# Packed bfloat16 constants in two loads, an earlier query load, more zero products and a later load of the first unit's rows

## The chip, the cores and the metric

The kernel runs on one core of a Trainium2 chip. The metric is the device time of one execution in microseconds (us). The core has the matmul engine (TensorE, PE in the rows; its weight loads are listed as PEld), VectorE (DVE), ScalarE (ACT), GpSimd (POOL) and SyncE (SP), which issues most of the transfers. Each engine works through its own instructions in order and meets the others only through semaphores.

## The reference, cut to what matters

```python
# 1. windowed attention, 2 batches x 8 heads x 768 positions x 64
k_sum = k.reshape(B, H, nb, 32, D).max(axis=3)
v_sum = v.reshape(B, H, nb, 32, D).mean(axis=3)
scores = concat(where(|i - j| < 16, q @ k.T / 8, -1e9), q @ k_sum.T / 8 + log(32))
x = softmax(scores) @ concat(v, v_sum)          # 1536 tokens x 512
# 2. mixture of 8 experts, one expert a token
logits = x @ w_gate;  e = argmax(logits);  gate = softmax(logits)[e]
y = gate * (relu(x_e @ w1[e]) @ w2[e])          # 512 -> 1024 -> 512
# 3. a dense block
h = y @ w_in                                    # 512 -> 2048
out = elu(h) @ w_out                            # 2048 -> 512
```

## The kernel before, in words

The order of all instructions is written out by hand. There are three phases. The first does the attention in 24 steps (12 tiles of 128 positions, two head groups `g` each; the loop over `n`, with `steps[n] = (i, g)`); the second does the experts in units of 384 rows; the third does the dense block in groups of 384 rows.

**A step of attention.** `stage_s` writes the mask into PSUM (a matmul of `ident_b` by the mask, L536), adds the logarithm (L538) and adds 16 score products of the queries `qts[i]` (L543). `stage_x` takes the maximum on DVE (L555 to L562) and the exponentials on ACT (L567). One step later `stage_t` transposes (L584) and two steps later `stage_o` multiplies by the values (L595, then L606 on DVE). After the stages of step `n` come the gate functions of earlier tiles (lists EARLY, MID and LATE), then `late(n)`, which prepares what comes: keys of later tiles, loads, weights.

**The opening.** SP issues the keys of pairs 0 and 1, the constants `cst` (1045 columns of four bytes by 128 rows), the keys of pairs 2 and 3, the queries of tile 0, four parts of the values of batch 0 (`load_vt`, 384 KB each), the queries of tile 1 and the windows of values. Meanwhile PE does WARM products of a zero tile (L752). ACT turns five constants into bfloat16 (`ident_b` L758, three masks L760, `logs` L761), and DVE a sixth (`tri_b`, L813, in `late(0)`). In step 1 and 2 the means of blocks of values are formed: sums on DVE (L911) and POOL (L909), products with `means` (`block_means`, L503), and in between zero products (`keep_clock`, L523); DVE and ACT then copy the means into the value windows (`put_means`, L508 and L509). DVE's `late(1)` converts the capacity (L819) before the first of these copies.

**From attention to the first unit.** Every tile's gate sends its 128 rows into a DRAM buffer `xdisp`, by an indirect store from POOL (`put`, L723; `gate_6` calls it). The first unit is the expert of token 0; `first_unit` is a generator whose pieces (`fill_pe`) are put between instructions of the last steps. It begins with transposes of the rows `XROW0` (L272). `load_rows` (L224) fetches them from `xdisp` in three transfers on SP in `late(X_AT)`; the first of them waits for all puts made so far. A put that comes after it in the program waits for the load, since both touch `xdisp`. In `late(22)`, `load_rows` (if X_AT is 22) stands ahead of the loads of later weights, and behind `gate_6(7)`, which puts tile 7.

**Conversions.** Both weights of the dense block arrive as 64-bit numbers; 32 chunks are turned into float32 on DVE in three instructions each (L406, L409, L400), and after the third the next chunk's load is issued on SP (L381). Chunks 0 to 5 are popped one instruction at a time in `stage_x` and `stage_o` (`fill_in`). What is left, and chunks 6 to 10, stand in the list `conv_tail`. It is popped at numbered places: at place `p` the entry `POINTS[p]` gives ten times the number of pieces of the first unit, plus the number of conversion instructions. Places 0 to 9 lie in steps 22 and 23, 10 to 30 behind the entries of `tail` (place 8 follows `gate_4(9)`, 19 follows `gate_3(10)`, 20 follows `gate_1(11)`), and 31 to 33 in the code that makes the lists of units. What is left of `conv_tail` then is popped in `rest_of_first` (`aside`), one for each piece.

Of the kernel before, what the change touches and what calls it, by code (L numbers as in the profile page):

```python
# [11 lines left out]
BF16 = mybir.dt.bfloat16  # L12
# [11 lines left out]
NB = S // BLK  # L24
# [4 lines left out]
P = 128  # L29
TQ = 64  # L30
WK = TQ + 2 * WIN
NK = WK + NB
# [19 lines left out]
def _consts():  # L52
# [4 lines left out]
    def add(name, a):  # L57
# [3 lines left out]
        cols.append(full)  # L61

    p = np.arange(P)
    add("ident", np.eye(P, dtype=np.float32))
    q = p[:, None] % TQ
    n = np.arange(WK)[None, :]
# [3 lines left out]
    for name, ok in (("mid", band), ("first", first), ("last", last)):  # L70
        m = np.zeros((P, NK), np.float32)
        half = (p[:, None] < TQ) == (name == "first")
        m[:, :WK] = np.where(np.where(half, ok, band), 0.0, NEG)
        add(name, m)

# [5 lines left out]
    for r in (0, D):  # L81
        m[r : r + 3] = np.array(parts, np.float32)[:, None]
    add("logs", m)
    m = np.zeros((P, NK), np.float32)
    m[p[: S // 8], WK + p[: S // 8] // (BLK // 8)] = 1.0 / BLK
    add("means", m)
    add("tri", (p[:, None] < p[None, :]).astype(np.float32))
    add("rev8", np.broadcast_to(E - np.arange(E, dtype=np.float32), (P, E)))
# [23 lines left out]
def moe_chain_kernel(  # L112
# [32 lines left out]
    wg = cp.tile([P, KD, E], F32, name="wg")  # L145
    tri_b = cp.tile([P, P], BF16, name="tri_b")
    ones_b = cp.tile([P, P], BF16, name="ones_b")
# [198 lines left out]
    W_AT = (9, 11, 13, 15, 17, 19, 21, 23)  # L346
    X_AT = 20
    A_AT = (15, 21)
    POINTS = (0, 0, 0, 0, 1, 1, 0, 0, 30, 0, 11, 11, 0, 1, 0, 22, 0, 22, 0, 30, 10, 10, 0, 0, 10, 0, 10, 0, 0, 0, 0, 20, 40, 53)
    WARM = 23  # L350
    PROLOGUE = 2
# [70 lines left out]
    with ExitStack() as att:  # L422
# [87 lines left out]

        masks = fx.tile([P, 3, NK], BF16, name="masks")
        ident_b = fx.tile([P, P], BF16, name="ident_b")
        logs = fx.tile([P, 4, NB], BF16, name="logs")
        OPS = BANK[4].rearrange("p (g u d) -> p g u d", g=2, u=4)
# [17 lines left out]
        def stage_s(i, g):  # L532
            t = i % TPB
            mask = masks[:, 1 if t == 0 else 2 if t == TPB - 1 else 0, :]
            sp = BANK[g][:, 0 : 4 * NK].rearrange("p (u n) -> p u n", u=4)
# [3 lines left out]
                sp[:, :, WK:NK], ones_b[g * D : g * D + 3, :], logs[g * D : g * D + 3], start=False, stop=False  # L539
            )  # L540
            for u in range(4):
                for j in range(2):
                    nc.tensor.matmul(  # L543
                        sp[j * TQ : (j + 1) * TQ, u, :],
                        qts[i][rows, u, j * TQ : (j + 1) * TQ],
                        kws[i][rows, u, j, :],
                        start=False,
                        stop=(u == 3),
                    )
# [190 lines left out]
        load_k(0, 1, 1)  # L740
        nc.sync.dma_start(cst, consts)
        load_k(0, 2, 1)
        load_k(0, 3, 1)
        load_q(0)
        for m in range(4):
            load_vt(0, m)
        load_q(1)
        load_vx(0)
        load_vx(1)

        for _ in range(WARM):
# [5 lines left out]
        block_max(0, 1)  # L757
        nc.scalar.copy(ident_b, ident)  # L758
        for n, name in enumerate(("mid", "first", "last")):
            nc.scalar.copy(masks[:, n, :], C(name))  # L760
        nc.scalar.copy(logs, C("logs").unsqueeze(1).to_broadcast([P, 4, NB]))  # L761
        put_kw(0, nc.scalar.copy, slice(2, 4))
# [40 lines left out]
        def late(n):  # L803
# [6 lines left out]
            if n == 0:  # L810
                nc.sync.dma_start(wg, w_gate.rearrange("p (k e) -> p k e", e=E))
                nc.sync.dma_start(cap_raw, capacity.to_broadcast([P, 1]))
                nc.vector.tensor_copy(tri_b, C("tri"))  # L813
                nc.vector.memset(ones_f, 1.0)
# [629 lines left out]
```

## Time and profile before

| what | us |
|---|---|
| median of 3 runs | 445.79 |
| lowest and highest of these | 445.54 and 449.44 |
| the profiled execution: its own time | 446.14 |
| the profiled execution: span of its trace | 444.5 |

The mean granted clock of TensorE is 0.970 of full speed in the profiled execution. The span runs from the first to the last instruction; the rest of the execution's own time (1.64 us) lies around it. Starts in the rows count from the begin of the span.

A row of the timeline has the start, the duration of all instructions that were merged into it, the engine (SPq is SP's queue), the source line, the operation, the tiles (out<-in), shapes, the count, and in brackets how long the engine had been idle before it and what ended that. A row of a table by stretches has the stretch, then for each engine its busy time and number of instructions, then the granted clock as a share of full speed (1.00 is 2.4 GHz, 0.50 is 1.2 GHz), the mean busy share of the 16 DMA engines, and GB/s.

### The profile page before, as it was taken

Reading aid. Unit: us, or ns where it says so; the run is one execution under the profiler, and the core shown is the slowest. Engines: PE = TensorE matmul, PEld = TensorE weight load, DVE = VectorE, ACT = ScalarE, POOL = GpSimd, SP = SyncE. Lnnn points to the kernel's source line nnn. Section 1 sums busy time; section 2 is a strip of 40 time slices with the busy share of each in tenths; the row PEclk is TensorE's granted clock in tenths of the full one; section 3 lists DMA queues with packets and bytes.
Section 4 is the critical chain, followed back from the end, with each engine's and each line's share of the span. In section 5 each row is a group of like instructions: output and inputs, shape, how many; then the busy total and the mean of one; then the engine's idle time right before and its main releaser. Section 6 shows DMA issues by size and latency. Waiting matters only on the chain. (4 is left out here: it accounts for less than half of the span.)

```text
span 444.5 us, 8062 instructions
## 1 busy us (share of the span) xinstructions
PE 417.4 (94%) x2756; PEld 360.9 (81%) x2756; DVE 344.1 (77%) x764; ACT 232.5 (52%) x580; POOL 72.6 (16%) x147
## 2 busy tenths in 40 slices
PE   7799999995989889999899999999999999999994
PEld 3467767774979789999788988788998998998983
DVE  4567979784767959967987999999777877777871
ACT  3356788782464336456257677655434334434331
POOL 2201954733312001101000000000300000200002
PEclk9889999995899989999999999999999999999998
DMA  8958888679466898978853900020100020100001
GB/s 267 246 151 253 263 291 268 226 217 350 153 207 202 99 207 230 396 225 123 318 190 112 352 3 0 1 71 1 71 2 0 1 73 0 72 1 1 0 2 73
DMA packets 33782, 63.54 MB, mean 143 GB/s; under 512 B 5877, under 2 KB 16117, under 8 KB 33728
## 3 DMA queue, kind: packets, MB, share of 16 engines
q1 hardware_dynamic: 30320, 51.87, 41.0%
q0 software_dynamic: 3408, 11.03, 6.4%
q8 instruction: 25, 0.41, 0.4%
q14 instruction: 29, 0.24, 0.2%
HBM read 50.26 MB, written 13.42 MB: 143 GB/s over the span
## 5 line engine op out<-in xcount | busy, mean ns | idle before, releaser
L1263 PE MATMUL bank<-wout_r,hh 128*128 128x512 f32 x144 | 57.1, 396 | 1.2 <-DVE wout_r L1243 1.2
L567 ACT ACTIVATE ex<-bank,nm 128x120 f32<-128x120 f32 x96 | 33.4, 366 | 9.2 <-DVE nm L560 6.7
L1311 ACT ACTIVATE hf<-bank 128x384 f32<-128x384 f32 x24 | 11.8, 490 | 41.4 <-PE bank L261 41.4
L1263 PEld LDWEIGHTS bank<-wout_r,hh 128*128 128x128 f32 x144 | 27.0, 188 | 6.7 <-DVE wout_r L1243 2.3
L1311 ACT ACTIVATE xrow<-bank 128x384 f32<-128x384 f32 x24 | 11.7, 489 | 38.3 <-PE bank L261 38.3
L543 PE MATMUL bank<-spare,qt 64*64 64x120 f32 x384 | 26.4, 280 | 3.0 <-DMA qt<-in_q_dram 3.0
L1263 PE MATMUL bank<-w2raw_r,hl 128*128 128x512 f32 x72 | 28.7, 399 | 0.0
L1263 PE MATMUL bank<-w2raw_r,hh 128*128 128x512 f32 x72 | 28.4, 394 | 0.0
L261 PE MATMUL bank<-yh,win_r 128*128 128x384 f32 x128 | 27.0, 337 | 0.0
L261 PE MATMUL bank<-xh,wal 128*128 128x384 f32 x112 | 24.9, 344 | 1.0 <-DVE wal L241 1.0
L1275 POOL DMA_INDIRECT out_dram<-raw,idt x6 | 6.1, 1024 | 118.6 <-ACT raw L1272 118.0
L261 PE MATMUL bank<-xh,wah 128*128 128x384 f32 x112 | 25.5, 350 | 0.0
L261 PE MATMUL bank<-xl,wah 128*128 128x384 f32 x112 | 24.5, 340 | 0.0
L543 PEld LDWEIGHTS bank<-spare,qt 64*64 64x64 f32 x384 | 20.7, 139 | 4.4 <-POOL oobs L818 2.7
L281 PE MATMUL bank<-hh,wbl 128*128 128x384 f32 x96 | 20.9, 339 | 3.1 <-DVEq L1379 2.0
L261 PEld LDWEIGHTS bank<-yh,win_r 128*128 128x128 f32 x128 | 22.8, 188 | 0.4
L281 PE MATMUL bank<-hh,wbh 128*128 128x384 f32 x96 | 20.9, 338 | 2.0 <-PEq L1379 1.1
L1158 ACT ACTIVATE hf<-bank 128x384 f32<-128x384 f32 x16 | 7.9, 493 | 27.1 <-PE bank L261 23.8
L1326 DVE SCALAR_TENSOR_TENSOR xrow<-hf,xrow 128x384 f32<-128x384 f32 x24 | 13.4, 556 | 11.1 <-ACT hf L1313 9.1
L261 PEld LDWEIGHTS bank<-xh,wal 128*128 128x128 f32 x112 | 20.3, 193 | 1.5 <-DVE wal L241 1.4
L261 PEld LDWEIGHTS bank<-xh,wah 128*128 128x128 f32 x112 | 20.6, 196 | 0.6
L723 POOL DMA_INDIRECT xdisp<-xr,idx x12 | 15.6, 1298 | 33.8 <-DVE sel L982 11.7
(255 smaller groups left out, 1127.6 us busy)
## 6 DMA issues: line engine op xcount, KB each, us to landing
w1raw<-in_moe_w_dram SPq DMA_DIRECT2D x12, 512.0 KB
w2raw<-in_moe_w_dram SPq DMA_DIRECT2D x12, 512.0 KB
raw<-in_moe_w_out_dram POOLq DMA_DIRECT2D x12, 512.0 KB, 7.7
raw<-in_moe_w_in_dram SPq DMA_DIRECT2D x10, 512.0 KB
qt<-in_q_dram SPq DMA_DIRECT2D x12, 256.0 KB
w2raw<-in_v_dram SPq DMA_DIRECT2D x8, 384.0 KB
rows<-in_moe_w_in_dram SPq DMA_DIRECT2D x6, 512.0 KB
yr<-ydT SPq DMA_DIRECT2D x4, 768.0 KB
```

The lines of the kernel that those rows point to most:

```text
L261: nc.tensor.matmul(hp, wa[a][:, kk, cols], xa[b][:, kk, :], start=(n == kk == 0), stop=(n == 2 and kk == KD - 1))
L281: nc.tensor.matmul(ACC[d][:, 0:SLOT], wb[a][:, jj, d * P : (d + 1) * P], hb[b], start=(f == 0 and n == 0), stop=(f == NF1 - 1 and n == 2),)
L543: nc.tensor.matmul(sp[j * TQ : (j + 1) * TQ, u, :], qts[i][rows, u, j * TQ : (j + 1) * TQ], kws[i][rows, u, j, :], start=False, stop=(u == 3),
L567: nc.scalar.activation(ex[:, u, :], sp[:, u, :], AF.Exp, bias=nm[:, u : u + 1], scale=0.125, accum_out=den[:, u : u + 1])
L723: ins = nc.gpsimd.indirect_dma_start(xdisp, bass.IndirectOffsetOnAxis(ap=idx, axis=0), xr, None, bounds_check=E * REG - 1, oob_is_err=Fals ...
L1158: nc.scalar.activation(hf, hp, AF.Relu)
L1263: nc.tensor.matmul(ACC[s], ga[a][:, cols], wb[b][:, jj, :], start=(f == n == 0), stop=(f == NF2 - 1 and n == 2),)
L1275: put = nc.gpsimd.indirect_dma_start(out, bass.IndirectOffsetOnAxis(ap=IDT[g % 3][:, s : s + 1], axis=0), OBS[(NS * g + s) % len(OBS)], No ...
L1311: nc.scalar.activation(x, hp, AF.Relu, scale=-1.0)
L1326: nc.vector.scalar_tensor_tensor(z, x, 1.0, z, op0=ALU.add, op1=ALU.mult)
```

## The change

Constants: the identity in bfloat16, the three masks, the logarithm (already repeated four times) and the triangle are packed on the host, two bfloat16 numbers to a column, and used where they lie; the six conversions on the chip are gone. The array has 889 columns in place of 1045. Its first 604 are loaded where the whole was loaded before; the other 285 by a second transfer behind the value windows. The queries of tile 1 are loaded behind the second part of the values, not the fourth. WARM is 26, not 23, and five zero products stand ahead of the scores of tile 1's first group, behind its mask. X_AT is 22, not 20. POINTS has two more conversion instructions at place 19 and one more at place 20.

```diff
+    def add_b(name, a):
+
+        bits = np.ascontiguousarray(a, np.float32).view(np.uint32)
+        halves = ((bits + 0x8000) >> 16).astype(np.uint16)
+        add(name, np.ascontiguousarray(halves).view(np.uint32).view(np.float32))
+
     add("ident", np.eye(P, dtype=np.float32))
+    add_b("ident_b", np.eye(P, dtype=np.float32))
...
-        add(name, m)
+        add_b(name, m)
...
-    add("logs", m)
+    add_b("logs", np.tile(m, (1, 4)))
...
-    add("tri", (p[:, None] < p[None, :]).astype(np.float32))
+    add_b("tri", (p[:, None] < p[None, :]).astype(np.float32))
+    CONST_COLS["first part"] = (0, sum(c.shape[1] for c in cols))
...
-    tri_b = cp.tile([P, P], BF16, name="tri_b")
+    tri_b = C("tri").bitcast(BF16)
...
-    X_AT = 20
+    X_AT = 22
     A_AT = (15, 21)
-    POINTS = (0, 0, 0, 0, 1, 1, 0, 0, 30, 0, 11, 11, 0, 1, 0, 22, 0, 22, 0, 30, 10, 10, 0, 0, 10, 0, 10, 0, 0, 0, 0, 20, 40, 53)
-    WARM = 23
+    POINTS = (0, 0, 0, 0, 1, 1, 0, 0, 30, 0, 11, 11, 0, 1, 0, 22, 0, 22, 0, 32, 11, 10, 0, 0, 10, 0, 10, 0, 0, 0, 0, 20, 40, 53)
+    WARM = 26
...
-        masks = fx.tile([P, 3, NK], BF16, name="masks")
-        ident_b = fx.tile([P, P], BF16, name="ident_b")
-        logs = fx.tile([P, 4, NB], BF16, name="logs")
+        masks = [C(name).bitcast(BF16) for name in ("mid", "first", "last")]
+        ident_b = C("ident_b").bitcast(BF16)
+        logs = C("logs").bitcast(BF16).rearrange("p (u n) -> p u n", u=4)
...
+            if (i, g) == (1, 0):
+                keep_clock(5)
             for u in range(4):
...
-        nc.sync.dma_start(cst, consts)
+        _, n = CONST_COLS["first part"]
+        nc.sync.dma_start(cst[:, 0:n], consts[:, 0:n])
         load_k(0, 2, 1)
         load_k(0, 3, 1)
         load_q(0)
         for m in range(4):
             load_vt(0, m)
-        load_q(1)
+            if m == 1:
+                load_q(1)
         load_vx(0)
         load_vx(1)
+        nc.sync.dma_start(cst[:, n:], consts[:, n:])
...
-        nc.scalar.copy(ident_b, ident)
-        for n, name in enumerate(("mid", "first", "last")):
-            nc.scalar.copy(masks[:, n, :], C(name))
-        nc.scalar.copy(logs, C("logs").unsqueeze(1).to_broadcast([P, 4, NB]))
...
-                nc.vector.tensor_copy(tri_b, C("tri"))
```

## Rows read from the trace of the kernel before

**Rows 1.** The page, engines: busy time, share of the span, instructions
```profile
PE 417.4 (94%) x2756; PEld 360.9 (81%) x2756; DVE 344.1 (77%) x764; ACT 232.5 (52%) x580; POOL 72.6 (16%) x147
```
**Rows 2.** Table by stretches of 1 us, in the opening
```profile
17.00:18.00 1.00, 0.00 (x0) 0.00 (x0) 0.06 (x1) 0.00 (x0) 0.94 (x4) 1.00 1.00 211
18.00:19.00 1.00, 0.06 (x2) 0.10 (x3) 0.96 (x2) 0.00 (x0) 0.97 (x3) 0.60 1.08 270
```
**Rows 3.** Timeline of the opening, 0 to 25 us
```profile
1.09 0.87 SPq L459 DMA_DIRECT2D rows<-in_k_dram  x2
...
2.60 7.80 PE L752 MATMUL bank<-warm 128*120 128x512 bf16 x23 [2.60 <-ACT warm L736]
...
5.59 0.33 ACT L445 COPY spare<-rows 128x160 f32<-128x160 f32 x1 [3.04 <-DMA rows<-in_k_dram]
...
7.51 0.30 ACT L758 CAST ident_b<-cst 128x128 bf16<-128x128 f32 x1 [1.22 <-DMA cst<-in_consts_dram]
...
7.77 2.18 PEld L752 LDWEIGHTS <-warm 128*120 128x120 bf16 x10 [0.20 <-issue]
...
17.94 0.69 DVE L911 TENSOR_TENSOR w2raw<-w2raw 96x512 f32<-96x512 f32 x1 [2.75 <-DMA w2raw<-in_v_dram]
...
18.66 1.63 DVE L911 TENSOR_TENSOR w2raw<-w2raw,w2raw 96x512 f32<-96x512 f32 x2
...
18.94 1.87 PE L543 MATMUL bank<-spare,qt 64*64 64x120 f32 x16 [2.57 <-DMA qt<-in_q_dram]
...
22.07 0.15 DVE L819 CAST cap<-cap_raw 128x1 f32<-128x1 int32 x1 [1.24 <-DMA cap_raw<-in_moe_capacity_dram]
...
22.91 1.91 PE L503 MATMUL bank<-w2raw,cst 96*120 96x512 f32 x2
...
24.86 0.70 DVE L508 COPY spare<-bank 24x512 f32<-24x512 f32 x1 [2.64 <-PE bank L503]
```
**Rows 4.** Timeline of steps 20 to 23, 84 to 108 us
```profile
90.88 1.20 POOL L723 DMA_INDIRECT xdisp<-xr,idx  x1 [0.78 <-ACT es L586]
...
94.28 0.69 DVE L400 SCALAR_TENSOR_TENSOR win<-raw,win 128x512 uint32<-128x512 uint32 x1
...
96.61 1.52 SPq L224 DMA_DIRECT2D rows<-xdisp  x3
...
98.22 0.38 SPq L381 DMA_DIRECT2D raw<-in_moe_w_in_dram  x1
98.52 0.74 ACT L707 ACTIVATE xr<-xt,gt 128x512 f32<-128x512 f32 x1
...
102.60 1.09 POOL L723 DMA_INDIRECT xdisp<-xr,idx  x1 [6.48 <-DMA rows<-xdisp]
...
104.42 0.43 DVE L406 TENSOR_SCALAR win<-raw 128x512 uint32<-128x512 uint32 x1 [3.78 <-DMA raw<-in_moe_w_in_dram]
...
107.94 0.17 PE L680 MATMUL bank<-oh,tri_b 128*128 128x8 bf16 x1 [4.13 <-DVE oh L666]
...
107.99 1.52 PE L272 MATMUL bank<-cst,rows 128*128 128x128 f32 x6
```
**Rows 5.** Instructions of line L723, the puts: from issue to landing
```profile
DMA to landing us min/median/max: 3.2/4.8/6.1
```
**Rows 6.** Timeline of the last tiles' gates, 119 to 134 us
```profile
123.35 1.23 DVE L241 TENSOR_TENSOR wal<-w1raw,wah 128x1024 fp32r<-128x1024 f32 x1 [1.01 <-ACT wah L240]
...
126.93 0.18 PE L680 MATMUL bank<-oh,tri_b 128*128 128x8 bf16 x1 [0.52 <-DVE oh L666]
...
133.61 0.29 PE L991 MATMUL bank<-prod,ones_f 32*1 32x77 f32 x2 [1.26 <-DVE prod L984]
```
**Rows 7.** Timeline of the first unit's second half, 138 to 158 us
```profile
139.78 1.23 DVE L293 TENSOR_TENSOR wbl<-w2raw,wbh 128x1024 fp32r<-128x1024 f32 x1 [2.28 <-ACT wbh L292]
...
156.83 0.98 PE L281 MATMUL bank<-hh,wbl 128*128 128x384 f32 x4 [2.02 <-DVEq L1379]
```
**Rows 8.** Table by stretches of 10 us, same stretch
```profile
140.00:150.00 10.00, 9.67 (x61) 9.40 (x60) 9.80 (x17) 6.72 (x13) 0.73 (x1) 1.00 1.00 183
```

More of the change, by code (lines that the diff above doesn't have):

```diff
@@ L533, in stage_s @@
             t = i % TPB
-            mask = masks[:, 1 if t == 0 else 2 if t == TPB - 1 else 0, :]
+            mask = masks[1 if t == 0 else 2 if t == TPB - 1 else 0]
             sp = BANK[g][:, 0 : 4 * NK].rearrange("p (u n) -> p u n", u=4)
```

## The prediction

> **What bounds the kernel now.** I read the engine table first, then the table by stretches, then the timeline wherever PE's busy time in a stretch fell. PE is busy for 94% of the span [rows 1], and each engine takes its work in a fixed order, so whatever lets PE go on sooner is worth its full length as long as PE stays the last one. Time is therefore to be found only where PE stands still or runs at the lower clock, and the change touches three such places.
>
> The first is the opening. PE waits 2.57 us for the queries of tile 1 and begins its scores at 18.94; meanwhile the granted clock falls from 1.00 towards 0.50 (2.4 and 1.2 GHz) [rows 2, 3]. At the lower clock PE reaches the products of the block means at 22.91, and DVE copies them at 24.86, which all later steps wait for [rows 3].
>
> The second is the end of attention. SP issues the load of the first unit's rows at 96.61, when the put of tile 6 (POOL, 90.88) has landed. Until then SP holds the load of conversion chunk 6, whose buffer was free at 94.97 (L400) but which goes out at 98.22; so DVE waits 3.78 us for it until 104.42, its gate of tile 9 is late, and PE waits 4.13 us until 107.94. POOL, too, stands for 6.48 us, since the put of tile 7 may not pass the load [rows 4]. PE's next work, the transposes of the rows, starts at 107.99.
>
> The third is the first unit. DVE is busy for 9.80 of the 10 us from 140 on, and PE waits 2.02 us for it before 156.83 [rows 7, 8].
>
> **The change part by part.** I count in the time of the trace before; a minus is a gain.
>
> *Opening.* Six casts go (the first is 0.30 on ACT [rows 3]); ACT and DVE had idle time there, so by themselves they are worth nothing. The first transfer of constants has 604 columns of 512 bytes (128 rows of four bytes), 226 KB less than 1045. The queries of tile 1 move ahead of two parts of the values, 393 KB each. So 226 + 786 = 1012 KB less stand ahead of them; at some 240 GB/s, the mean of 211 and 270 [rows 2], they land 4.2 us sooner, at 14.7. PE gets to these scores later than that, so the wait of 2.57 us goes. What is late next? The last part of the values has 262 - 226 = 36 KB more ahead of it than before, 0.15 us, so DVE's sums start at 18.1 in place of 17.94 and end at 18.1 + 0.69 + 1.63 = 20.4. The two products then take half of 1.91 at the full clock, 0.95, and end at 21.4. But DVE must convert the capacity ahead of the copy, and this waited for its transfer until 22.07 [rows 3]. That transfer has 80 KB less ahead of it, though one descriptor list more (the second constants): 0.0 to 0.33 us sooner. I take 22.0 for it and 22.15 for the copy of the means. The gain is 24.86 - 22.15 = 2.7 us. The bounds: 3.4 us, if the capacity came in time (21.4), and 0.8 us, if the clock fell after all: then the scores (1.87), five zero products (5 x 0.44) and the two of the means (1.91) at the lower clock, from 18.1 on (below), put the copy at 24.1.
>
> The zero products: 23 take 7.80 us, and the weight loads of the last ten come every 2.18 / 10 = 0.22 us, which is their price at the full clock [rows 3]. Three more are 0.65 us, five more 1.1 us. Before, PE was idle for 2.57 us until 18.94, so it was free at 16.37; now it comes to tile 1's scores at 16.37 + 0.65 + 1.1 = 18.1, has them done by 19.05 (half of 1.87), and after the five zero products that stood there before (1.1) it is at the means at 20.15, just ahead of 20.4: all eight are hidden behind the values. If that cover went, they would cost 1.75 us. The second part of the constants makes POOL wait for its columns in `late(1)` until about 22; behind it stand only fills and keys of step 6, which have time.
>
> *Rows of the first unit.* At step 22 the load stands behind `gate_6(7)`, so it also waits for the put of tile 7. That put needs its rows from ACT (98.52 + 0.74 = 99.26), so POOL starts it at 99.35; the 6.48 us of POOL's wait go. SP no longer holds chunk 6: its load goes out at about 95, DVE's wait of 3.78 us goes, and the gate of tile 9 is ready at about 104.2. So far PE would have 107.94 - 104.2 = 3.8 us. But the transposes then need the rows. The put of tile 6 took 96.61 - 90.88 = 5.73 us from its start to SP's release, and the load 102.60 - 96.61 = 5.99 us from its first issue to the last landing [rows 4]. The puts land 3.2 to 6.1 us after issue, 4.8 in the middle [rows 5]. I take the middle, since little else is under way then: the load goes out at 99.35 + 4.8 + 0.1 = 104.25 and lands at 110.24, so PE begins the transposes 2.2 us later than the 107.99 of before. The three transfers also hold back SP's next ones (four chunks and a part of the weights) by 5 us; these are first needed after 122, and cost nothing. Bounds: a landing of 6.1 gives 111.54 and +3.5. From below, 3.2 for the put and, for the load, the 4.5 us in which the keys came in the opening (issued at 1.09, used at 5.59 [rows 3], 786 KB against the rows' 793) give 99.35 + 3.2 + 0.1 + 4.5 = 107.15 and -0.8.
>
> The Trainium skill, page "DMA: Bandwidth & Descriptors", section "Anatomy of one DMA — SWDGE (gpsimd) path", speaks for the lower bound: a DMA issued by GpSimd takes about 2.0 us plus its bytes at 436 GB/s, so an estimate for the 264 KB of a put is 2.6 us. By it the load would go out at 102.1, the rows land at 108.1, and this part cost 0.1 us in place of 2.2. No put in this trace landed in under 3.2 us, so the sum stays with the rows.
>
> *Three conversions moved.* L400 takes 0.69 and L406 0.43 [rows 4]; with L409 taken as L400, of the same form, the three are 1.8 us of DVE. They leave the first unit, where DVE is full until PE's wait of 2.02 us ends [rows 7, 8]: -1.8 there. They come in between the gates of tiles 10 and 11. At 123.35 DVE has L241 until 124.58, then the three; the gate of tile 11 slips by up to 1.8 us, and PE, which waits for it already at 126.93 (0.52 us), slips by as much. But PE then also waits 1.26 us at 133.61 [rows 6] for a buffer that POOL clears after a put; that wait doesn't depend on these DVE instructions and swallows 1.26 of the 1.8. What is left is +0.5. Together -1.3; the bounds are -1.8 (DVE has room at 124) and +1.8 (the first unit's wait has another cause, and the wait at 133.61 moves along).
>
> *Sum.* -2.7 + 2.2 - 1.3 = -1.8 us, against the profiled execution's own time: 446.14 - 1.8 = 444.3. That execution is 0.35 us above the median of the runs, so the predicted time is 444.0. Behind 158 us PE is busy nearly throughout, and I let the shift go through to the end.
>
> **The rivals.**
> 1. *The rows come in time.* With the DMA engines idle, put and load take their lower bounds. For it: chunk 6 and the weights go out at 95, so nothing is queued at 99.35. Against it: the same load found an idle queue at 96.61 too and took 5.99 us [rows 4]. Then -2.7 - 0.8 - 1.3 = -4.8: 441.0 on the median's footing. The skill's rule above comes out near it, at -2.7 + 0.1 - 1.3 = -3.9, 441.9.
> 2. *The conversions hold up the last gate* (slower). Place 19 lies between two tiles whose gates run through DVE one after the other, and PE waits there already [rows 6]. If the whole 1.8 us stays and nothing comes back at 156.83, the sum is -2.7 + 2.2 + 1.8 = +1.3: 447.1. It decides from the point where PE's wait ahead of L680 of tile 11 grows by more than 1.3 us while the one ahead of L991 stays. Against it: DVE has 0.2 us left between 140 and 150 [rows 8].
> 3. *The opening gains little*: the clock falls all the same, as some short waits of PE stay. For it: it fell within 2 us of PE's last product [rows 2, 3]. Against it: the idle 2.57 us go. Then -0.8 + 2.2 - 1.3 = +0.1: 445.9.
>
> **How the numbers follow.** The forecast has 0.45, the rivals 0.2, 0.2 and 0.15. About 1% (4.5 us) is what a measurement of this kernel can tell from no change. Below 441.3 lie most of rival 1 and a small part of the forecast: 0.2. Above 450.3 there is only what I have overlooked: 0.06. The rest, 0.74, is within 1%. The range goes from 440.0 (the opening's and rival 1's bounds together, -3.4 - 0.8 - 1.8, are 439.8) to 448.5 (the slower rival with the upper bound for the rows, +3.5, is 448.4). The forecast's own range is 442.5 to 445.7.
>
> **What would show it.** Right: no wait of PE for `qt` at 18, a clock of 1.00 from 10 to 95 us, the copy of the means near 22 behind L819; L723 of tile 7 at once behind its ACT scale, but L272 waiting some 6 us for the rows; a longer wait at the last gate's L680, none at L991, and a shorter one near 156. Wrong: L272 right behind L680 of tile 9 (then rival 1), the clock at 0.50 before 25 (rival 3), or L819 long past before the means are ready, which makes the opening better than I say.

## The result, and the profile after

The changed kernel took 444.88 us (median of 20 executions, 437.58 to 451.53) where the kernel before took 445.71 (20 executions, 442.89 to 451.96). The ratio is 0.988 with a 95% interval of 0.984 to 0.992; it leaves slow executions out, the two medians alone give 0.998, and both profiles of the changed kernel used below are of longer executions of it (447.56 and 444.77 us, where 11 of 32 took 437.6 to 441.1). On a second chip the same pair gave 1.005 (1.000 to 1.010; medians 444.60 and 442.87), and the kernel before set against itself on a third gave 1.007 (1.003 to 1.011). So a ratio closer than 1% to one says nothing here. The forecast was 444.0, no change that can be measured, and so it came out. What the single steps did must be read from the traces, by the time between landmarks.

The table has five stretches of PE's timeline, in us. *Means* is DVE's first copy of the block means (L508 before, L516 after). *Rows* goes from the first gate product of tile 9 (tiles counted from 0), which waits 0.70 us for ScalarE (L637, L647), to the first output product behind the transposes of the rows (L595, L605). *Gate* goes from there to the gate of tile 11 (last L680, L690), *first unit* from there to the last layer-2 wait (L281, L289 behind the branch). *Second unit* goes from there to PE's wait of 0.77 or 0.78 us for `wout_r` (L1263, L1271). Ahead of *rows* and behind *second unit*, what is left is the same within 0.3 us in all of them (73.3 to 73.6, and 201.4 to 201.5), but for step 20 alone (experiment 2), where the first of these is 78.8.

| kernel | means | rows | gate | first unit | second unit | span |
|---|---|---|---|---|---|---|
| before, first profile | 24.86 | 13.59 | 14.94 | 29.90 | 86.20 | 444.5 |
| before, again | 19.98 | 13.85 | 15.05 | 29.66 | 89.01 | 442.5 |
| before, casts on GpSimd | 23.42 | 12.86 | 15.68 | 29.54 | 89.28 | 445.5 |
| changed, first profile | 20.95 | 15.43 | 16.73 | 28.39 | 89.72 | 445.9 |
| changed, again | 21.94 | 13.92 | 16.83 | 28.37 | 87.48 | 443.2 |
| changed, one more copy on ScalarE | 21.10 | 14.73 | 16.75 | 26.92 | 82.32 | 436.5 |
| step 21 | 20.53 | 10.02 | 16.71 | 28.37 | 88.28 | 438.6 |
| step 21, five copies, conversions last | 21.30 | 10.91 | 15.62 | 28.49 | 82.89 | 433.9 |

The clock is in these lengths too. In the changed kernel's profiles it is at 1.00 up to the copy of the means, where in the first profile of before it fell, and yet its mean over the execution is 0.968 and 0.971, against 0.970 there: behind the last gate it falls where before it held, and in *rows* it is low for longer. In *second unit* it falls behind the last layer-2 wait in nine of all fourteen profiles, of the kernel before too, and costs about 1.7 us there; no experiment explains in which.

*The opening.* The timelines of PE and DVE after, which answer to [rows 3]:

```profile
16.52 1.29 PE L531 MATMUL bank<-warm 128*120 128x512 bf16 x5
17.74 1.04 PE L553 MATMUL bank<-spare,qt 64*64 64x120 f32 x16
18.71 1.29 PE L531 MATMUL bank<-warm 128*120 128x512 bf16 x5
19.84 1.02 PE L511 MATMUL bank<-w2raw,cst 96*120 96x512 f32 x2
...
17.00 0.69 DVE L919 TENSOR_TENSOR w2raw<-w2raw 96x512 f32<-96x512 f32 x1 [1.60 <-DMA w2raw<-in_v_dram]
20.76 0.15 DVE L827 CAST cap<-cap_raw 128x1 f32<-128x1 int32 x1 [1.02 <-DMA cap_raw<-in_moe_capacity_dram]
20.95 0.70 DVE L516 COPY spare<-bank 24x512 f32<-24x512 f32 x1
```

PE's wait for `qt` is gone, the scores take 1.04 us in place of 1.87 and the products of the means 1.02 in place of 1.91: the clock stayed at 2.4 GHz. The copy follows the conversion of the capacity (L827) at once; the products of the means had ended 0.05 us before that. It stands 3.9 us sooner than in the first profile of before.

*The rows.* POOL, SP and PE after, which answer to [rows 4]:

```profile
95.90 1.09 POOL L733 DMA_INDIRECT xdisp<-xr,idx  x1 [3.96 <-ACT xr L717]
...
90.81 0.35 SPq L389 DMA_DIRECT2D raw<-in_moe_w_in_dram  x1
...
99.12 1.49 SPq L232 DMA_DIRECT2D rows<-xdisp  x3
...
99.98 0.17 PE L690 MATMUL bank<-oh,cst 128*128 128x8 bf16 x1 [1.15 <-DVE oh L676]
101.88 0.47 PE L280 MATMUL bank<-cst,rows 128*128 128x128 f32 x1 [1.71 <-DMA rows<-xdisp]
102.58 0.47 PE L280 MATMUL bank<-cst,rows 128*128 128x128 f32 x1 [0.23 <-DMA rows<-xdisp]
106.43 1.12 PE L280 MATMUL bank<-cst,rows 128*128 128x128 f32 x4 [3.38 <-DMA rows<-xdisp]
```

POOL no longer stands 6.48 us for the load, chunk 6 goes out at 90.81 ahead of it, and the gate of tile 9 comes early. But the load waits for the put of tile 7, and PE for the rows: 1.71 + 0.23 + 3.38 = 5.3 us. (The L690 at 99.98 is the ninth of twelve, that of tile 8 when the tiles are counted from 0 as for the puts; the prediction and the expectations call it the gate of tile 9.)

*Gate and units.* PE after, which answers to [rows 6] and [rows 7], and one wait that the kernel before has not:

```profile
126.40 0.18 PE L690 MATMUL bank<-oh,cst 128*128 128x8 bf16 x1 [1.31 <-DVE oh L676]
...
152.08 0.95 PE L289 MATMUL bank<-hh,wbh 128*128 128x384 f32 x4 [0.32 <-PEq L1387]
154.79 1.52 PE L289 MATMUL bank<-hh,wbl 128*128 128x384 f32 x4 [1.76 <-DVEq L1387]
174.05 0.96 PE L269 MATMUL bank<-xh,wah 128*128 128x384 f32 x4 [3.48 <-ACT wah L248]
```

The gate's wait grew from 0.52 to 1.31 us, the one at L999 went, and those of layer 2 shrank. In the second unit PE now waits 3.48 us for `wah`, the rounded first weights that ScalarE makes at L248; this is the line that the experiments had to explain.

### The profile page after: what moved, and what is told of

Same layout as the page of the kernel before. It is cut to its first block, busy times and chain, and to the rows that moved or that the text cites. A ratio compares the mean times of both kernels' runs of the same rounds, so it can differ in the third digit from the quotient of the medians.

```text
span 445.9 us, 8069 instructions
## 1 busy us (share of the span) xinstructions
PE 419.7 (94%) x2764; PEld 363.8 (82%) x2764; DVE 344.2 (77%) x763; ACT 232.0 (52%) x575; POOL 70.3 (16%) x147
## 5 line engine op out<-in xcount | busy, mean ns | idle before, releaser
L1271 PE MATMUL bank<-wout_r,hh 128*128 128x512 f32 x144 | 57.1, 397 | 1.2 <-DVE wout_r L1251 1.2
L1319 ACT ACTIVATE hf<-bank 128x384 f32<-128x384 f32 x24 | 11.7, 489 | 41.6 <-PE bank L269 41.6
L1271 PEld LDWEIGHTS bank<-wout_r,hh 128*128 128x128 f32 x144 | 27.0, 188 | 6.8 <-DVE wout_r L1251 2.3
L1271 PE MATMUL bank<-w2raw_r,hl 128*128 128x512 f32 x72 | 28.8, 400 | 0.0
L1271 PE MATMUL bank<-w2raw_r,hh 128*128 128x512 f32 x72 | 28.3, 393 | 0.0
L269 PE MATMUL bank<-xl,wah 128*128 128x384 f32 x112 | 25.6, 352 | 0.0
L553 PE MATMUL bank<-spare,qt 64*64 64x120 f32 x384 | 24.9, 269 | 0.0
L289 PE MATMUL bank<-hh,wbl 128*128 128x384 f32 x96 | 21.3, 345 | 1.8 <-DVEq L1387 1.8
L289 PE MATMUL bank<-hh,wbh 128*128 128x384 f32 x96 | 21.3, 344 | 1.2 <-PEq L1393 0.8
L289 PE MATMUL bank<-hl,wbh 128*128 128x384 f32 x96 | 21.2, 343 | 0.0
L596 ACT COPY es<-bank 120x512 f32<-120x512 f32 x24 | 14.1, 589 | 13.1 <-PE bank L594 12.6
L565 DVE TENSOR_REDUCE mx<-bank 128x4 f32<-128x480 f32 x24 | 15.7, 653 | 6.8 <-PE bank L553 6.6
```

The lines of the kernel that those rows point to most:

```text
L269: nc.tensor.matmul(hp, wa[a][:, kk, cols], xa[b][:, kk, :], start=(n == kk == 0), stop=(n == 2 and kk == KD - 1))
L289: nc.tensor.matmul(ACC[d][:, 0:SLOT], wb[a][:, jj, d * P : (d + 1) * P], hb[b], start=(f == 0 and n == 0), stop=(f == NF1 - 1 and n == 2),)
L553: nc.tensor.matmul(sp[j * TQ : (j + 1) * TQ, u, :], qts[i][rows, u, j * TQ : (j + 1) * TQ], kws[i][rows, u, j, :], start=False, stop=(u == 3),
L565: nc.vector.tensor_reduce(mx, sp, axis=AX.X, op=ALU.max)
L596: nc.scalar.copy(es, ep)
L1271: nc.tensor.matmul(ACC[s], ga[a][:, cols], wb[b][:, jj, :], start=(f == n == 0), stop=(f == NF2 - 1 and n == 2),)
```

## The experiments

Twelve kernels ran, each timed in five rounds beside the kernel before. "Changed" is the kernel after the change, unaltered.

**1. The changed kernel again.** No edit.

> The changed kernel once more, unaltered, as the control for the runs beside it. My theory: the steps show again at the same places (copy of the means near 21.0, transposes of the first unit's rows waiting some 5 us in all from 100 on, gate of tile 11 near 126.4, no wait at L999), and the profiled execution ends near 440, because ScalarE's 7.5 us without work at 165 to 173, which the first profile of it showed, is no part of the change. Rival: that idle time belongs to the change (to the loads that it moved) and stands again at the same place.

Measured: 444.60 us (12 executions). The opening and the rows came again (means at 21.94, transposes waiting 1.34 + 0.76 + 1.47 us). The gate is at 126.00, and L999 doesn't wait. But ScalarE stood still again, from 164.98 to 171.58, and PE waited 2.52 us for `wah`. My theory fell on the point that mattered: this idle time belongs to the change.

**2. The rows' loads at step 20.**

```diff
-    X_AT = 22
+    X_AT = 20
```

> The rows' loads go back to step 20, the rest of the change stays. My theory (the later place costs 1.6 us): DVE again waits some 3.8 us for conversion chunk 6 and POOL some 6.5 us before the put of tile 7, the gate of tile 9 is ready some 4 us later, but the transposes follow it at once, without a wait for rows, and the first product behind them (L605) starts near 108.0 in place of 109.7: 1.5 to 2 us faster than the changed kernel. Rival (the later place is where the gain is): L605 starts later than 109.7 and the time is 2 us or more longer than the changed kernel's.

Measured: 443.42 us, so no difference in the time. The waits came back as expected (POOL 6.74 us ahead of the put of tile 7, DVE 4.12 us for chunk 6), and the transposes followed the gate without a wait for rows. L605 stood at 115.20, since this execution's opening was slow (below); from the gate product of tile 9 it took 13.64 us, where seven profiles with step 22 took 13.3 to 15.7, 14.4 in the mean. By this one profile the later place costs 0.8 us, half of what I expected; for the rival, by which it gains, nothing speaks.

**3. The rows' loads at step 21.**

```diff
-    X_AT = 22
+    X_AT = 21
```

> The rows' loads go out at step 21, between the two. My theory: the load then waits for the put of tile 6 alone, which lands near 92.6, chunk 6 isn't held up by it, the gate of tile 9 stays near 100, and PE's wait of 5.3 us for the rows goes nearly whole: L605 starts near 104.7, and the time is 4 to 5 us shorter than the changed kernel's. Rival (the transfer is what takes its 7 us, since it shares the DMA engines with chunks and weights): 2 to 3 us of the wait stay and the gain is 2 us or so; or POOL's put of tile 7 waits again and makes a later tile late.

Measured: 438.62 us, ratio to before 0.988 (0.980 to 0.996). SP and PE of this kernel:

```profile
90.39 0.35 SPq L389 DMA_DIRECT2D raw<-in_moe_w_in_dram  x1
92.55 1.51 SPq L232 DMA_DIRECT2D rows<-xdisp  x3
...
99.56 0.17 PE L690 MATMUL bank<-oh,cst 128*128 128x8 bf16 x1 [1.93 <-DVE oh L676]
...
100.42 0.85 PE L280 MATMUL bank<-cst,rows 128*128 128x128 f32 x6
...
103.85 1.12 PE L605 MATMUL bank<-rows,es 120*64 120x64 f32 x16
```

Chunk 6 goes out ahead of the load, as at step 22, and the load waits for tile 6 alone, as at step 20. It has landed when PE comes. The first product is at 103.85 (I said 104.7). One step earlier than the change put it, the move is worth 2.6 to 3.5 us (*rows* takes 10.0 to 10.9 us in the three kernels with step 21, 13.5 with step 20); at step 22 it gives all of that to the wait for the put of tile 7. That put, which the program then has behind the load, is later at step 21, at 98.06 in place of 95.90; *gate* is no longer for it (16.71 us), so no cost shows.

**4. The three conversions back at their old places.**

```diff
-    POINTS = (..., 22, 0, 32, 11, 10, 0, 0, 10, ...)
+    POINTS = (..., 22, 0, 30, 10, 10, 0, 0, 10, ...)
```

> The three conversions go back to places 19 to 21 of the old list, the rest of the change stays. My theory (worth 1.3 us net where they are now): the gate of tile 11 is ready 0.8 to 1.8 us sooner (L690 near 125.1, hardly a wait), L999 waits again about 1 us for the buffer that POOL clears, PE's wait for DVE ahead of the first unit's products grows by about 1.8 us, and the time is 1 to 2 us longer than the changed kernel's. Rival (the conversions now hold up the last gate): nothing is lost behind L999 and the time is 1 to 1.8 us shorter.

Measured: 445.07 us, as the changed kernel within what can be told. PE of this kernel:

```profile
124.22 0.18 PE L690 MATMUL bank<-oh,cst 128*128 128x8 bf16 x1 [0.52 <-DVE oh L676]
...
130.92 0.29 PE L999 MATMUL bank<-prod,ones_f 32*1 32x77 f32 x2 [1.28 <-DVE prod L992]
...
151.15 0.97 PE L289 MATMUL bank<-hh,wbh 128*128 128x384 f32 x4 [1.12 <-PEq L1387]
154.13 0.96 PE L289 MATMUL bank<-hh,wbl 128*128 128x384 f32 x4 [2.00 <-DVEq L1387]
```

The waits stand where they stood before, to 0.02 us. The gate is ready 1.8 us sooner (14.99 us in place of 16.8), and all of it is lost again behind it. *Gate* and *first unit* together take 44.90 us here and 45.12 and 45.20 in the changed kernel: the moved conversions gain nothing, where I had 1.3. Where it went shows in the windows behind the gate of the changed kernel run again, and of this one (columns: stretch, its length, busy time of PE, its weight loads, DVE, ACT and POOL, the granted clock, the DMA's share and GB/s):

```profile
125.00:130.00 5.00, 3.80 (x19) 3.24 (x20) 3.50 (x20) 2.39 (x5) 0.57 (x1) 0.74 0.52 206
130.00:135.00 5.00, 5.00 (x27) 4.61 (x27) 3.88 (x12) 1.92 (x3) 3.25 (x6) 0.91 0.03 4
```

```profile
125.00:130.00 5.00, 4.64 (x28) 4.05 (x27) 2.62 (x11) 3.65 (x6) 0.95 (x1) 1.00 0.17 65
130.00:135.00 5.00, 4.08 (x24) 3.97 (x25) 4.26 (x12) 0.66 (x2) 3.63 (x6) 1.00 0.13 26
```

Behind the longer wait at the gate the clock falls: 0.26 and 0.09 of five microseconds each are missing, 1.75 us of full speed, which at 1.2 GHz is 3.5 us. It does so in seven of the nine profiles that have the conversions at places 19 and 20, and in none of the other five. In the two in which it does not (experiments 6 and 12, though their waits at the gate are 2.15 and 2.19), the first unit's stretch is 27.22 and 26.92 in place of 28.4. Why it holds there stayed open.

**5. The kernel before again.** No edit.

> The kernel before, unaltered, profiled on the chip of the runs beside it, as the control for their landmarks. My theory: the landmarks of its first profile come again within 1 us (copy of the means near 24.9 behind a fallen clock, product L595 after the rows' transposes near 112, gate of tile 11 near 126.9, the first unit's last layer-2 wait near 156.8, ScalarE's conversion L240 near 167.4 without a wait). Rival: its opening is as variable as the changed kernel's (values landed between 16.8 and 18.2 in five profiles), and the copy of the means comes 1 us or more sooner or later.

Measured: 447.48 us (443.53 to 449.30); the profiled execution, at 444.15, was one of the three fastest of twelve. Its opening:

```profile
16.80 1.04 PE L543 MATMUL bank<-spare,qt 64*64 64x120 f32 x16 [1.39 <-DMA qt<-in_q_dram]
...
18.90 1.02 PE L503 MATMUL bank<-w2raw,cst 96*120 96x512 f32 x2
...
19.98 0.70 DVE L508 COPY spare<-bank 24x512 f32<-24x512 f32 x1
```

The queries landed 2.1 us sooner than in [rows 3], PE waited 1.39 us in place of 2.57, the clock did not fall, and the copy of the means was 4.9 us sooner, with nothing changed. The rival holds: the opening of before has two forms. Over the first 20 us the DMA engines moved 274 GB/s in this execution and 255 in the first profile. The changed kernel kept its clock at 256 and 257, and lost it at 242 (experiment 2, clock 0.50 from 30 to 40). So the change seems to let the good form stand at a slower DMA; that was not tried by itself, and the rate alone doesn't decide, since before with its casts on GpSimd lost its clock at 272 (experiment 11). Where before has the good form anyway, nothing is gained (20.5 to 22.8 against 19.98 in the profiles that kept their clock up to the copy).

**6. Five small copies on ScalarE, where the five casts had been.**

```diff
         block_max(0, 1)
+        pad = fx.tile([P, 8], F32, name="pad")
+        for n in range(5):
+            nc.scalar.copy(pad[:, n : n + 1], ident[:, n : n + 1])
         put_kw(0, nc.scalar.copy, slice(2, 4))
```

> The changed kernel with five copies of one column on ScalarE in the place of the five casts that the change took out, so that ScalarE has as many instructions as before. Theory F (the wait of PE for wah at 168 to 172 comes from fetching ScalarE's instructions: with five fewer, the next block is fetched later, behind the small stores of the ids and the rows): the wait of 2.2 to 3.5 us ahead of L269, which stands in four profiles of the changed kernel's family and in none of before, goes; the fetch is served near 157 in place of 169, and the time is 2 to 3 us shorter than the changed kernel's. Rival (the wait comes from the later weights or rows of the second unit): the wait stays at 2 us or more, and the time is the changed kernel's.

Measured: 439.70 us (438.69 to 441.17), ratio to before 0.988 (0.984 to 0.993). ScalarE went on at 162.51 without a wait, and PE waited for no `wah`. The span is 439.0 against 443.2 and 445.9 of the changed kernel.

**7. Step 21 and the five copies together.** Both edits above.

> Rows at step 21 and the five small copies on ScalarE together. Theory F: the transposes follow the gate of tile 9 as in the kernel with step 21 alone (first product behind them near 104), the wait of 2.6 us for wah goes, and the time is some 2.5 us below that kernel's and 6 to 8 us below the changed kernel's. Rival: the wait stays, and the time is that of step 21 alone.

Measured: 438.73 us (435.99 to 439.44), ratio 0.985 (0.980 to 0.990): no wait for `wah`, *rows* 10.65. The span is 437.3, 1.3 us under that of step 21 alone and 5.9 to 8.6 under the two of the changed kernel. The medians of the two lie 0.1 us apart, on different chips, whose kernel before differed by 3.3 us, so they decide nothing. The trace gives the price of the wait best here, since the clock falls alike in both second units: that stretch is 85.46 us, against 88.28 at step 21 alone, 2.8 us less.

**8. The queries of tile 1 behind the values again.**

```diff
         for m in range(4):
             load_vt(0, m)
-            if m == 1:
-                load_q(1)
+        load_q(1)
         load_vx(0)
```

> The queries of tile 1 go back behind the last part of the values; the shorter constants and the zero products stay. My theory by the measured order (PE is free for these scores at 17.6, with the eight zero products): the queries land near 18.0, PE waits 0.5 us or less, the clock stays at 1.00, the values come 1.5 us sooner, and the copy of the means still waits for the capacity, near 21.8: within 0.5 us of the changed kernel. Rival (the early queries make the opening's gain): PE waits 1.5 us or more for qt, the clock falls to 0.50 before 25, and the copy of the means is at 24 or later, 2 to 3 us longer.

Measured: 441.23 us (437.23 to 445.54). PE came to the scores at 17.06 without a wait, the clock stayed at 2.4 GHz and the copy of the means was at 20.60. The order of the queries is not what gains, in this profile; what is left of the change does it without them. The wait for `wah` was there, 2.85 us.

**9. No added zero products** (with the five copies of experiment 6).

```diff
-    WARM = 26
+    WARM = 23
-            if (i, g) == (1, 0):
-                keep_clock(5)
```

> The kernel with the five small copies on ScalarE, without the eight zero products that the change added (23 in place of 26 at the start, none ahead of tile 1's scores). My theory: they are hidden while the values are on their way, so the copy of the means stays at 20.5 to 22, and the median at 439.7, within 1 us; the scores of tile 1 start near 16.4 or when the queries land. Rival (they are what holds the clock): PE stands still some 2 us longer before the means, the clock falls to 0.50 between 22 and 35 in this profile or in part of the runs, the copy of the means is at 23 or later, and the median is 2 us or more longer.

Measured: 443.19 us (438.14 to 446.30). Windows and PE's timeline of its opening:

```profile
10.00:15.00 5.00, 3.86 (x38) 2.59 (x38) 3.62 (x10) 2.25 (x12) 0.43 (x1) 0.88 1.05 244
15.00:20.00 5.00, 5.00 (x21) 2.62 (x21) 1.75 (x3) 1.94 (x9) 2.01 (x3) 0.50 1.04 235
...
11.41 1.04 PE L551 MATMUL bank<-spare,qt 64*64 64x120 f32 x16 [1.14 <-DVE spare L459]
...
13.80 3.77 PE L511 MATMUL bank<-w2raw,cst 96*120 96x512 f32 x4
...
24.55 0.70 DVE L516 COPY spare<-bank 24x512 f32<-24x512 f32 x1 [1.90 <-PE bank L511]
```

In this profile the rival was right; five of the 12 executions took 438.1 to 440.5 us, so it need not be so in all. PE reaches the first scores sooner, waits 1.14 us for their keys, and the clock falls at 13.8; the copy is at 24.55. The eight products cost nothing that shows, as I had said, but they are not ballast either: with them the same scores began at 11.44 without a wait in the first profile after. Which of the eight hold the clock was not separated; this fall came ahead of the place of the five (the scores of tile 1 start at 18.94), so of the eight only the three at the start can have been missing there.

**10. Conversions behind the gates** (with step 21 and the five copies): from places 19 and 20 to the last.

```diff
-    POINTS = (..., 0, 32, 11, 10, 0, 0, 10, 0, 10, 0, 0, 0, 0, 20, 40, 53)
+    POINTS = (..., 0, 30, 10, 10, 0, 0, 10, 0, 10, 0, 0, 0, 0, 20, 40, 56)
```

> Rows at step 21, the five small copies on ScalarE, and the three conversions taken from places 19 and 20 to the last place (behind prod, where DVE had 2 to 3 us free in each 5 us from 125 to 140). My theory: the gate of tile 11 is ready 1.8 us sooner after the tile before it (15.0 us from the first product behind the rows' transposes to L690, in place of 16.8), the clock no longer falls to 0.50 behind it, L1002 waits some 1.1 us again, and the first unit's layer 2 keeps the shorter waits (0.32 and 1.75): 1.5 to 2 us less than with the conversions at 19 and 20, 436 to 437. Rival (DVE is the bound from 140 on, and the conversions' place before it doesn't matter, or they hold up the unit list): the wait ahead of the first unit's layer 2 grows by 1 us or more, and the time is that of the kernel with the conversions at 19 and 20, 438.7.

Measured: 436.14 us (median of 6, 434.20 to 444.87), ratio to before 0.978 (0.973 to 0.984): the fastest of all. The windows:

```profile
120.00:125.00 5.00, 4.79 (x32) 4.10 (x31) 3.50 (x19) 2.85 (x7) 0.00 (x0) 1.00 0.63 247
125.00:130.00 5.00, 3.46 (x21) 3.04 (x20) 3.05 (x13) 1.46 (x3) 3.64 (x5) 1.00 0.02 4
...
128.06 0.29 PE L1002 MATMUL bank<-prod,ones_f 32*1 32x77 f32 x2 [1.54 <-DVE prod L995]
```

The clock stays at 1.00, L1002 waits 1.54 us, the layer-2 waits keep their short form (0.32 and 1.76). *Gate* and *first unit* together take 44.1 us, against 45.4 in experiment 7: 1.3 us gained, a little less than I said. Experiments 6 and 12, whose clock held with the conversions at 19 and 20, have 44.0 and 43.7, so what is gained is most likely the clock. The span, 433.9 against 437.3, also lacks the clock's fall in the second unit.

**11. The kernel before, its five casts on GpSimd.**

```diff
-        nc.scalar.copy(ident_b, ident)
+        nc.gpsimd.tensor_copy(ident_b, ident)
...
-            nc.scalar.copy(masks[:, n, :], C(name))
-        nc.scalar.copy(logs, C("logs").unsqueeze(1).to_broadcast([P, 4, NB]))
+            nc.gpsimd.tensor_copy(masks[:, n, :], C(name))
+        nc.gpsimd.tensor_copy(logs, C("logs").unsqueeze(1).to_broadcast([P, 4, NB]))
```

> The kernel before with its five casts moved from ScalarE to GpSimd: ScalarE has five instructions fewer, as in the changed kernel, and nothing else of the change is done. Theory F: the wait for wah shows itself here too (2 to 3.5 us ahead of L261 some 15 to 18 us behind the first unit's last layer-2 wait, ScalarE idle for 4 to 7 us before its L240), with the fetch of ScalarE's block served some 12 us later than in the kernel before. Rival (the wait comes from the moved loads of the rows or the conversions): L240 goes on without a wait as in both profiles of before.

Measured: 446.73 us, as before. L240 went on at 165.32 without a wait. Theory F failed as I had put it: five instructions fewer are not enough. (Its clock fell too, at 12.3, behind a wait of 0.79 us ahead of tile 0's scores; the copy was at 23.42.) Counted in the traces, ScalarE's branch hint ahead of the units (L1082, L1090; it tells the engine where a coming branch may go) is its instruction 413 in both profiles of before, 408 in this kernel, 412 in the four with five copies, and 407 in all six profiles in which ScalarE stands still. The change takes out six of ScalarE's instructions, five casts and one wait on a semaphore. If the place decides, the border lies between 407 and 408.

**12. One small copy on ScalarE.** As experiment 6, with `range(1)`: instruction 408.

> The changed kernel with a single copy of one column added on ScalarE in the opening. Theory F, made sharper: by the traces ScalarE's branch hint ahead of the units is its instruction 407 in the six kernels that wait for wah and 408, 412 or 413 in the seven that don't, so the place of the block's border among ScalarE's instructions decides, and one instruction more is enough: the fetch is served near 155, before the small stores of the ids, L248 goes on at 162 to 164 without a wait, PE doesn't wait for wah, and the time is 3 to 5 us shorter than the changed kernel's. Rival (it was the work of the five copies or the opening's timing that kept the wait away): ScalarE stands still for 4 to 7 us again, PE waits 2 us or more for wah, and the time is the changed kernel's.

Measured: 438.48 us (437.86 to 442.28), ratio to before 0.990 (0.984 to 0.995); span 436.5 against 443.2 and 445.9. The changed kernel's ratios were 0.988 and 1.005, on other chips, so the ratios don't tell the two apart; the trace does. ScalarE of the changed kernel run again, then of this one:

```profile
164.47 0.51 ACT L1167 CAST hh<-hf 128x384 fp32r<-128x384 f32 x1
171.58 1.04 ACT L248 CAST wah<-w1raw 128x1024 fp32r<-128x1024 f32 x1 [6.60 <-DMA xrow<-xdisp]
```

```profile
161.29 0.51 ACT L1170 CAST hh<-hf 128x384 fp32r<-128x384 f32 x1
161.71 1.05 ACT L248 CAST wah<-w1raw 128x1024 fp32r<-128x1024 f32 x1
```

One instruction of a few tenths of a microsecond in the opening takes away 6.6 us of ScalarE's standing still at 165, and with it PE's wait of 2.52 us. That is not the whole 6.7 us between the spans: *second unit* is 5.2 us shorter than in the changed kernel run again, of which 2.8 are the waits for `wah` and for `wal` behind it and 1.7 the clock, which fell there from 154 to 159 and not here; *first unit* is 1.45 us shorter, with the clock at 1.00 behind the gate. Kernels with five copies had both falls (experiments 7 and 9), so these are not shown to be the copy's doing. The DMA view shows what moved: the small queue of instruction packets (columns: queue and kind, packets, MB, share). First the changed kernel from 152 to 156, then from 169 to 171 us; from 156 to 169 its view has no row of that queue. Then the kernel with one copy from 152 to 156; from there to 171 it has none.

```profile
q14 instruction: 1, 0.01, 0.6%
...
q14 instruction: 1, 0.01, 1.0%
```

```profile
q14 instruction: 2, 0.02, 1.0%
```

By the DMA packets in the traces, with 408 or more the second packet follows the first of the pair by 0.7 to 2.1 us in all eight profiles, and with 407 by 14.4 to 15.6 us in five and 6.6 in that of experiment 2. In between lie SP's store of the ids (at 158.20 in the changed kernel: 1.5 KB in pieces of four bytes) and the three loads of the second unit's rows (at 160.53), which took 10.8 us to land. The windows of the changed kernel run again show what the DMA engines did meanwhile (the last two columns):

```profile
160.00:162.00 2.00, 2.00 (x13) 2.00 (x12) 1.10 (x3) 1.97 (x4) 0.00 (x0) 1.00 2.21 31
162.00:164.00 2.00, 2.00 (x13) 2.00 (x13) 1.97 (x3) 0.60 (x3) 0.00 (x0) 1.00 0.00 0
164.00:166.00 2.00, 2.00 (x14) 2.00 (x12) 2.00 (x5) 0.95 (x2) 0.00 (x0) 1.00 0.81 34
166.00:168.00 2.00, 2.00 (x13) 2.00 (x13) 1.46 (x3) 0.00 (x0) 0.17 (x1) 1.00 0.19 26
```

The DMA engines slow down in the kernel with one copy as well (15 to 34 GB/s from 160 to 166), but there the packet has come before. The packet that comes late is served only when they move again, and ScalarE goes on at 171.58, when the rows have landed too. The view doesn't say whose packet it is. That it is ScalarE's is inferred, from its moving with one instruction of ScalarE, and from this: in all six profiles ScalarE stops behind its instruction 395, and instruction 396 starts 1.29 us after the end of this packet in four of them (0.87 and 3.10 in the other two). Instruction 396 tests a semaphore and takes 17 ns, so once it had begun, no semaphore held it. The profile's view names the rows as the releaser, but in the kernel with one copy L248 begins at 161.71, with SP still issuing these loads.

The Trainium skill, page "Runtime: NRT & Kernel Launch", section "Instruction fetch mechanics", says that an engine's sequencer fetches its next block of instructions by a DMA of its own while it executes the present one, that the cost is mostly hidden, and that a taken branch breaks this. These runs fit the first point, by the packets above, and show an exception to the second: the wait stands 18 instructions behind the branch at L1387, and is 4.2 to 7.6 us of ScalarE in six profiles.

## Why the prediction was right in its number and wrong in its terms

The number held because errors met, which is luck. The rows cost 1.3 us less than I said, and a wait that the first profile of before had at 212 to 219, 1.8 us, went unforeseen; on the other side the conversions gained 1.3 less, and a wait of 2.5 us came that I had not seen. And that first profile had the bad form of an opening that has two.

- *Opening, -2.7.* Against the first profile of before it was -2.9 and -3.9. The mechanism was right: the wait for `qt` and the low clock went, the capacity is what is late next, and the zero products are hidden. The values and the capacity came 1.1 and 1.2 us sooner than I set them in the first profile (17.00 in place of 18.1, 20.76 in place of 22.0). What failed lay outside the steps: I took one execution's opening for that of the kernel. Experiment 5 had the copy at 19.98 without the change. So rival 3, the small gain, holds against the executions of before that keep their clock, though not for its reason. And in one profile each, the step came without the early queries, on which I had built it (experiment 8), and did not come without the zero products (experiment 9).
- *Rows later, +2.2.* The mechanism came as told, and the size was off: +0.9, from 13.5 in four profiles with step 20 to 14.4 in seven with step 22. Of the term, the put was mis-sized: I took 4.8 us for its landing and 0.1 more, and from its start to the load it was 3.1 to 3.6 us in seven profiles. The load took 5.2 to 7.3 us, where I had 5.99. The Trainium skill's rule, an estimate of 2.6 us for the put (page "DMA: Bandwidth & Descriptors", section "Anatomy of one DMA — SWDGE (gpsimd) path"), stood nearer than my row of the middle, yet no put came in that time either. Part of the spread may be the clock, which I left out here: its mean from 95 to 120 us lies between 0.66 and 0.80 in these eleven profiles. What I did not see at all was step 21.
- *Conversions, -1.3.* The gate slipped by 1.8 us, as forecast. Behind it the waits went by 1.26 at L991, 0.33 and 0.8 at layer 2 and 0.26 behind the branch, 2.65 together, where I had 3.06. I had set the whole 1.8 us against the last of these waits, the 2.02 us of [rows 7], and that one went by 0.26: with 1.8 us of DVE's work taken away, it is not this work that sets it. Then the clock at 1.2 GHz behind the longer gate wait took 1.2 to 1.5 us back. The term is 0.0: 44.9 us for *gate* and *first unit* together in both kinds, four and nine profiles. This is the step that failed most: I priced a longer wait of PE at its length and left the clock out, though in the opening I had counted with just that. Rival 2 was nearer to what happened at the gate, but its price of +1.8 was given back behind it.
- *Not in the sum.* ScalarE's late instructions, 2.2 to 3.5 us of PE in five of the six profiles that have them. I had put the casts that go at nothing, since ScalarE had idle time there; what mattered was the number of its instructions. Against that, the kernel before waits 1.8 to 4.1 us at 212 to 219 in its three profiles (L281 for `wbl`, L261 for `wal`, behind a chunk for which DVE waits 3.9 to 6.2 us), and the changed ones at most 0.4. Why these went is open; no run was made for it.

By the stretches of the table the changed kernel run again stands to the first profile of before at -2.9 - 0.2 (up to *rows*) + 0.3 + 1.9 - 1.5 + 1.3 = -1.1, and its span at -1.3. My sum was -1.8.

## What to carry to other kernels

A transfer that needs a put can be moved too late as well as too early: look for the step at which it neither holds up the queue behind it nor waits for one put more. A longer wait of PE can cost more than its length, by the clock behind it, and work taken off one engine's full stretch should go where no product waits for that engine (here behind `prod`). When a change removes instructions and a wait appears far away, look at the instruction packets before any theory on the data, and profile the unchanged kernel more than once, so that an opening with two forms isn't taken for one.

## What the runs showed of the hardware

The number of ScalarE's instructions ahead of a point, not their work, decided whether it stood still there for 4.2 to 7.6 us: at 407 it did in six profiles, at 408 to 413 it did not in eight, and one added copy took the wait away. Where the clock fell alike in both kernels, the wait was worth 2.8 us of the second unit (experiments 3 and 7). Behind a store of 1.5 KB in four-byte pieces the DMA engines moved 0 to 34 GB/s for eight microseconds with three loads of 258 KB issued, and these took 10.8 us, where three like them take 5.99 in [rows 4]. The same opening, unchanged, moved 255 GB/s in one execution and 274 in another, and the copies of the means stood 4.9 us apart, by a clock that fell in the one and held in the other. The clock fell behind waits of 0.79, 1.14 and 2.57 us in the opening and of 1.3 at the gate, and held behind 1.39 in the one place and 2.19 in the other: the length of the last wait alone doesn't tell.
